# Transposing a token block with VectorE squares and 32 on-chip transfers instead of TensorE, from the fifth block on

## The chip, the core and the metric

The program runs on one core of a Trainium2 chip. The core has five engines that each work through their own queue in order and wait for each other through semaphores: PE (TensorE, matmuls), DVE (VectorE), ACT (ScalarE), POOL (GpSimd) and SP (SyncE, which here only issues DMAs). The metric is the device time of one execution in microseconds (us). Before the change the median of 3 runs is 1261.0 us (1260.62 to 1261.91).

## What is computed

Three layers over 8192 tokens of 192 channels (`D`), cut to what matters:

```
w   = softmax(weight_gen)            # per token: 8 heads x 7 taps
x1  = sum over k of w[..., k] * x[token - 6 + k]     # causal convolution, 24 channels a head
xn  = x1 / sqrt(mean(x1^2) + 1e-6) * rms_g
y   = (silu(xn @ w_gate) * (xn @ w_val)) @ w_out     # hidden size 1536
h   = y @ w_in                                       # hidden size 2048
out = (h * sigmoid(1.702 h)) @ w_out2
```

## The kernel before, in words

The 8192 tokens lie as 128 partitions of 64 consecutive tokens (a run of tokens per partition). A *block* is 4 tokens of every partition, 512 tokens in all; there are 16 blocks, 0 to 15. For a block the convolution works with tokens on the partitions (`conv_ops`, L215): 7 multiplications (L226) and 6 additions (L259) of 128x768 on DVE, then the sum of squares on ACT (L269, four instructions, called `sq` in the code), the reciprocal root on POOL (L274 and L276, `root`), and the scaling `xr = acc * ri` on DVE (L280) with a copy of the last 64 channels on ACT (L281).

The matmuls need channels on the partitions, so the block is transposed (`transpose_x`, L291). From block 3 on that is 16 PE transposes of 64x128 (L308) into two PSUM banks; `split` (L318) then reads PSUM and writes a high and a low part in float32r, on ACT (L324) and DVE (L325), for channels 0 to 127 (`xh`, `xl`) and for channels 128 to 191, which stand twice (`xsh`, `xsl`). All matmuls are made of high and low parts, and each takes 64 of the 128 partitions, upper and lower half in alternation, two at a time.

The work on PE is a list of *units*, written (layer, block, number). A unit (1, b, m) makes one 128-wide piece of gate and value of block b (12 a block); a unit (2, b, i) makes two pieces of the second hidden layer (8 a block). Each unit also holds "down" matmuls into the banks `a` and `b` with the hidden pieces of units before it. The hidden pieces come from PSUM over ACT (`silu`, and the high part `h`) and DVE (the product `p` in layer one, and the low part `l`, L435 and L455). From block 2 on the list reads, for each block b: (1, b, 4) to (1, b, 11), then (1, b+1, 0) to (1, b+1, 3), then (2, b, 0) to (2, b, 7). The low part of the even piece 2i of a layer-two unit i is used by the next unit, that of the odd piece by the one after (L698, L699).

When a PSUM bank passes from matmuls on one half of the partitions to matmuls on the other half, `handed` (L353) puts an empty instruction (a *word*) on POOL's queue that waits for the earlier matmul, and lets the later matmul wait for the word. A layer-two unit has six such words, the first before its fourth pair of matmuls.

The convolution of the coming block is handed out between the units. `some` (L579) records as much of a stream of DVE, ACT and POOL work as its cost, spread evenly until a due unit, asks for: half before the first low part of the unit (`second`), half before the second (`third`). The due unit hangs on `xt_at[b]`, the unit at which block b is transposed: L520 sets it to unit (1, b-1, 10). The convolution of block b starts at the transposition of block b-1 and is due two units before its own. The softmax weights are made for three blocks at once, so in front of blocks 4, 7, 10 and 13 stands a softmax: maximum and subtraction first, the exponential at unit (2, b-2, 2) (L668), and only then the rest of the softmax and the whole convolution (L678).

SP issues, per block, the load of the next x, and the two output DMAs of `Z` (L488), which scales the result of a block and adds its two halves (L495).

Of the kernel before, what the change touches and what calls it, by code (L numbers as in the profile page):

```python
# [18 lines left out]
P = 128  # L19
# [5 lines left out]
D = 192  # L25
DR = D - P
M1 = 12
# [3 lines left out]
BLOCKS = [4] * 16  # L31
# [6 lines left out]
SIG = 1.702  # L38
# [3 lines left out]
def gated_conv_mlp(ctx: ExitStack, tc: tile.TileContext, xp, wg, w1, wo1, w2, wo2, g, out):  # L42
    nc = tc.nc
    NB = len(BLOCKS)
    T0 = [sum(BLOCKS[:i]) for i in range(NB)]
    TM = max(BLOCKS)
    NM = TM * P
# [7 lines left out]
    xtp = ctx.enter_context(tc.tile_pool(name="xtp", bufs=2))  # L55
# [13 lines left out]
    gt = const.tile([P, 2], F32, name="gt")  # L69
# [81 lines left out]
    xrow = {}  # L151
    xT = {}
# [62 lines left out]
    def conv_ops(b):  # L215

        T = BLOCKS[b]
        Q = T * HEADS
        x = xch[b]
        wn = wn_of[b]  # L220
        xr = att.tile([P, T, 2 * P], F32, tag="xr", name=f"xr{b}")
        prod = xr.rearrange("p t c -> p (t c)")[:, 0:Q * GRP]
        ops = []

        def mul(eng, k, dst, j0=0, j1=T):
            eng.tensor_tensor(  # L226
                out=dst.rearrange("p (q g) -> p q g", g=GRP),
                in0=x[:, (k + j0) * D:(k + j1) * D].rearrange("p (q g) -> p q g", g=GRP),
                in1=wn[:, j0 * HEADS:j1 * HEADS, k:k + 1].to_broadcast([P, (j1 - j0) * HEADS, GRP]), op=ALU.mult)
        cost = 1.04 * Q * GRP + 70  # L230
        if b < 2:
            S = T // 2
            sums_of = [pacc.tile([P, NM], F32, tag=f"{n}{b}", name=f"{n}c_{b}") for n in "ab"]
            acc_of = [sums_of[j // S][:, (j % S) * D:(j % S + 1) * D] for j in range(T)]
        else:
            acc = att.tile([P, T, D], F32, tag="acc", name=f"acc{b}")
            acc_of = [acc[:, j] for j in range(T)]
        if b == 1:
            def tap(k):
                for i, ps in enumerate(sums_of):  # L240
                    tag = (("yh", "yl"), ("ysh", "ysl"), ("yh0", "yl0"))[k % 3][i]
                    pr = ytp.tile([P, NM], F32R, tag=tag, name=f"pr{k}_{i}").bitcast(F32)[:, :S * D]
                    mul(nc.gpsimd, k, pr, i * S, (i + 1) * S)
                    nc.tensor.matmul(ps[:, :S * D], ident, pr, start=k == 0, stop=k == TAPS - 1)
            ops += [(cost, lambda k=k: tap(k)) for k in range(TAPS)]
        elif b == 0:
            n = S * D

            def tap(k):
                for i, ps in enumerate(sums_of):  # L250
                    mul(nc.vector, k, prod[:, i * n:(i + 1) * n] if k else ps[:, :n], i * S, (i + 1) * S)
                for i, ps in enumerate(sums_of if k else ()):
                    nc.vector.tensor_tensor(out=ps[:, :n], in0=ps[:, :n], in1=prod[:, i * n:(i + 1) * n], op=ALU.add)
            ops += [(cost, lambda k=k: tap(k)) for k in range(TAPS)]
        else:
            total = acc.rearrange("p t d -> p (t d)")

            def add():
                nc.vector.tensor_tensor(out=total, in0=total, in1=prod, op=ALU.add)  # L259
            for k in range(TAPS):  # L260
                ops.append((cost, lambda k=k: mul(nc.vector, k, prod if k else total)))
                if k:
                    ops.append((cost, add))
        ss = sml.tile([P, T], F32, tag="ss", name=f"ss{b}")
        ri = sml.tile([P, T], F32, tag="ri", name=f"ri{b}")

        def sq():
            for j in range(T):
                nc.scalar.activation(out=xr[:, j, 0:D], in_=acc_of[j], func=AF.Square,  # L269
                                     accum_out=ss[:, j:j + 1])  # L270
        ops.append((1500, sq))

        def root():
            nc.gpsimd.tensor_scalar(out=ss, in0=ss, scalar1=1.0 / D, scalar2=1e-6,  # L274
                                    op0=ALU.mult, op1=ALU.add)
            nc.gpsimd.tensor_tensor(out=ri, in0=ss, in1=half[:, :T], op=ALU.pow)  # L276
        ops.append((500, root))

        def sc(j):
            nc.vector.tensor_scalar_mul(out=xr[:, j, 0:D], in0=acc_of[j], scalar1=ri[:, j:j + 1])  # L280
            nc.scalar.mul(out=xr[:, j, D:2 * P], in_=acc_of[j][:, P:D], mul=ri[:, j:j + 1])  # L281
        for j in range(T):
            ops.append((230, lambda j=j: sc(j)))
        xrow[b] = xr
        return ops

    def sums(b, nm):

        return [pacc.tile([P, NM], F32, tag=f"{n}{b % 2}", name=f"{n}{nm}{b}") for n in "ab"]

    def transpose_x(b, halves=False):  # L291

# [195 lines left out]
    def Z(b):  # L488
        N = BLOCKS[b] * P
        pa, pb = acc2.pop(b)  # L490
        za = zp.tile([P, NM], F32, tag="za", name=f"za{b}")
        zb = zp.tile([P, NM], F32, tag="zb", name=f"zb{b}")[0:DR]
        nc.scalar.mul(out=zb[:, :N], in_=pb[DR:P, :N], mul=1.0 / SIG)
        nc.scalar.mul(out=za[:, :N], in_=pa[:, :N], mul=1.0 / SIG)
        nc.vector.scalar_tensor_tensor(out=zb[:, :N], in0=pb[0:DR, :N], scalar=1.0 / SIG, in1=zb[:, :N],  # L495
                                       op0=ALU.mult, op1=ALU.add)
        c = T0[b] * P
        nc.sync.dma_start(out=out[0:P, c:c + N], in_=za[:, :N])
        nc.sync.dma_start(out=out[P:D, c:c + N], in_=zb[:, :N])
# [17 lines left out]

    xt_at = {0: -1, 1: pos[1, 1, 0], 2: pos[2, 1, PAIRS - 2]}
    for b in range(3, NB):
        xt_at[b] = pos[1, b - 1, M1 - 2]  # L520
    xt_by_pos = {v: k for k, v in xt_at.items()}
    group_of = {b0: gi for gi, (b0, b1) in enumerate(GROUPS)}


# [41 lines left out]
    def run_work(upto):  # L566
        for q in streams:
            while q and q[0][0] <= upto:
                q.popleft()[2]()
# [27 lines left out]
    with ExitStack() as order:  # L597
# [45 lines left out]
        for i, u in enumerate(units):  # L643
            kind, b, m = u
            if (kind, b, m) == (1, 2, 0):
                early.close()
                late = ctx.enter_context(tc.tile_pool(name="late", bufs=6))
                parts.append((late, late))
            run_work(i)
            late = []  # L650
            if i in xt_by_pos:
                split = transpose_x(nxt, nxt > 2)
                if nxt == 1:
                    split()
                else:
                    late.append(split)
                nxt += 1
                if nxt == 2:
                    start_at = pos[1, 1, 1]
                elif nxt < NB:  # L660
                    start_at = i
            if i == start_at:
                load_x(nxt)
                end = xt_at[nxt]
                gi = group_of.get(nxt)
                if gi is not None and gi >= 2:
                    pr, ex_hook, post_ops = softmax_ops(gi, sm[gi])
                    ex_at = i + 4 if gi == 2 else pos[2, nxt - 2, 2]  # L668
                    add_work(1, ex_at, pr)
                else:  # L670
                    add_work(1, end - 2, conv_ops(nxt))
                gi = group_of.get(nxt + 1)
                if gi is not None and gi >= 2:
                    sm[gi] = softmax_load(gi)
            if ex_hook and i == ex_at:
                ex_hook()
                ex_hook = None
                add_work(1, xt_at[nxt] - 2, post_ops + conv_ops(nxt))  # L678
            downs, after = [], []
            while pend and pend[0][0] <= i:  # L680
                _, D_, key = pend.popleft()
                d, f = D_(*key)
                downs.append(d)
                after += [f] if f else []
            second, third = (U1 if kind == 1 else U2)(b, m, lambda *ups: matmuls(ups, downs, kind == 2 and b < 2))
            todo = [share(k, i) / 2 for k in (0, 1)]
            some(todo)
# [67 lines left out]
```

## Time and profile before

| what | value |
|---|---|
| median of 3 runs | 1261.0 us |
| the profiled execution | 1261.79 us |
| its span, from the first to the last instruction | 1260.0 us |
| PE busy | 1225.8 us (97%) |
| DVE busy | 773.3 us (61%) |
| ACT busy | 662.7 us (53%) |
| POOL busy | 32.9 us (3%) |
| mean granted TensorE clock | 0.994 |
| chain that ended last | PE 89%, DVE 7%, ACT 2% |

The prediction works on the profiled execution, which is 0.8 us above the median. The busy time of PE counts an instruction to its end, and instructions overlap; PE's pace is read from the distance of starts. On DVE and ACT too, an instruction can start some 0.08 us before the end of the one ahead of it, so what one costs in a queue is the distance of starts.

### The profile page before, as it was taken

The numbers are of one execution on the slowest core, as the hardware profiler recorded it, in microseconds if no ns is written. First come the engines' busy times: TensorE is split into PE (matmuls) and PEld (weight loads), VectorE is DVE, ScalarE is ACT, GpSimd is POOL, SyncE is SP. The second block draws the span as 40 slices with busy tenths as digits, with TensorE's granted clock in tenths as the row PEclk, the third lists the DMA queues.
The fourth block names the chain that finished last, engine by engine and source line by source line (L and its number), as shares of the span: only waits on it lengthen the run. The fifth ranks groups of instructions, "written<-read, shape, count | busy, mean of one in ns | idle before, by whom it ended". The sixth has DMA issues, their size and how long they took to land.

```text
span 1260.0 us, 26630 instructions
## 1 busy us (share of the span) xinstructions
PE 1225.8 (97%) x10500; PEld 1073.5 (85%) x10500; DVE 773.3 (61%) x1270; ACT 662.7 (53%) x1345; POOL 32.9 (3%) x53
## 2 busy tenths in 40 slices
PE   5798999999999999999999999999999999999998
PEld 3676899988899998999998888888888898888886
DVE  8888957566746556674664667456466655645432
ACT  3565664564545456454545655445464554554553
POOL 4000000000000000000000000000000000000000
PEclk8899999999999999999999999999999999999999
DMA  5754502001000010100101010010100001000000
GB/s 196 228 180 151 164 27 67 33 1 45 2 26 32 1 45 1 45 1 2 56 2 45 1 45 2 1 56 1 45 2 17 29 1 46 1 14 2 1 14 13
DMA packets 16956, 51.70 MB, mean 41 GB/s; under 512 B 2112, under 2 KB 2496, under 8 KB 16832
## 3 DMA queue, kind: packets, MB, share of 16 engines
q1 hardware_dynamic: 16832, 50.01, 12.3%
q8 instruction: 82, 1.34, 0.4%
q14 instruction: 42, 0.34, 0.1%
HBM read 43.71 MB, written 6.29 MB: 40 GB/s over the span
## 4 chain that ended last, share of the span: by engine, by line
PE 89%; DVE 7%; ACT 2%; issue 1%; DMA 1%; SPq 0%; POOLq 0%; DVEq 0%
PE a L342 23%; PE ph L342 20%; PE pg L342 16%; PE b L342 16%; PE pv L342 13%; DVE l L435 1%; DVE p L431 1%; DVE dec_a L104 1%; DVE xr L226 1%; DVE dec_s L108 1%; DVE dec_s L98 1%; DMA x<-in_xp 1%; ACT h L432 0%; DVE zt L100 0%; DVE acc L259 0%
## 5 line engine op out<-in xcount | busy, mean ns | idle before, releaser
L342 PE MATMUL a<-h,o 64*128 64x512 f32 x1792 | 518.9, 392 | 0.4 <-POOLq L357 0.2
L342 PEld LDWEIGHTS a<-h,o 64*128 64x128 f32 x1792 | 329.3, 185 | 22.0 <-POOLq L357 1.1
L342 PE MATMUL a<-l,o 64*128 64x512 f32 x896 | 311.4, 393 | 2.2 <-DVE l L455 2.0
L342 PE MATMUL b<-l,o 64*128 64x512 f32 x896 | 311.0, 392 | 0.3 <-DVE l L435 0.3
L342 PE MATMUL b<-h,o 64*128 64x512 f32 x896 | 311.1, 393 | 0.0
L455 DVE TENSOR_TENSOR l<-p,h 128x512 fp32r<-128x512 f32 x256 | 176.0, 691 | 203.3 <-ACT p L449 202.3
L448 ACT ACTIVATE h<-ph 128x512 fp32r<-128x512 f32 x256 | 153.9, 601 | 227.0 <-PE ph L342 220.3
L342 PE MATMUL pv<-xh,w 64*128 64x512 f32 x768 | 242.8, 396 | 7.0 <-DVE p L431 6.6
L342 PE MATMUL pg<-xh,w 64*128 64x512 f32 x768 | 244.4, 396 | 1.3 <-ACT w L119 1.3
L342 PE MATMUL ph<-yh,w 64*128 64x512 f32 x1024 | 232.1, 391 | 0.0
L431 DVE TENSOR_TENSOR p<-p,pv 128x512 f32<-128x512 f32 x192 | 131.7, 686 | 144.7 <-PE a L342 100.4
L432 ACT CAST h<-p 128x512 fp32r<-128x512 f32 x192 | 119.1, 620 | 171.7 <-DVE p L431 171.7
L427 ACT ACTIVATE p<-pg 128x512 f32<-128x512 f32 x192 | 114.6, 597 | 161.2 <-PE pg L342 160.4
L435 DVE TENSOR_TENSOR l<-p,h 128x512 fp32r<-128x512 f32 x192 | 132.8, 692 | 98.5 <-ACT h L432 98.5
L342 PEld LDWEIGHTS a<-l,o 64*128 64x128 f32 x896 | 165.6, 185 | 18.3 <-DVE l L455 4.1
L342 PEld LDWEIGHTS b<-l,o 64*128 64x128 f32 x896 | 165.7, 185 | 13.5 <-DVE l L435 0.7
L342 PEld LDWEIGHTS b<-h,o 64*128 64x128 f32 x896 | 164.8, 185 | 9.8
L342 PEld LDWEIGHTS pv<-xh,w 64*128 64x128 f32 x768 | 140.4, 186 | 20.7 <-DVE p L431 9.7
L342 PEld LDWEIGHTS ph<-yh,w 64*128 64x128 f32 x1024 | 143.3, 185 | 15.1 <-POOLq L357 0.2
L449 ACT ACTIVATE p<-ph 128x512 f32<-128x512 f32 x256 | 154.0, 602 | 0.0
L342 PE MATMUL pv<-xl,w 64*128 64x512 f32 x384 | 150.9, 393 | 0.0
L342 PE MATMUL pg<-xl,w 64*128 64x512 f32 x384 | 150.5, 392 | 0.0
(101 smaller groups left out, 2134.9 us busy)
## 6 DMA issues: line engine op xcount, KB each, us to landing
x<-in_xp SPq DMA_DIRECT2D x15, 960.0 KB, 5.1
st<-in_w SPq DMA_DIRECT2D x20, 384.0 KB, 3.8
zt<-in_w SPq DMA_DIRECT2D x20, 384.0 KB, 3.4
st<-in_wo SPq DMA_DIRECT2D x14, 384.0 KB, 3.9
zt<-in_wo SPq DMA_DIRECT2D x14, 384.0 KB, 3.3
out_z<-za SPq DMA_DIRECT2D x16, 256.0 KB, 2.0
out_z<-zb SPq DMA_DIRECT2D x16, 128.0 KB, 2.3
wraw<-in_wg SPq DMA_DIRECT2D x4, 336.0 KB, 5.4
```

The lines of the kernel that those rows point to most:

```text
L98: nc.vector.tensor_scalar(out=t["s"], in0=hi, scalar1=-0x80000000, scalar2=4, op0=ALU.bitwise_and, op1=ALU.bitwise_or)
L104: nc.vector.scalar_tensor_tensor(out=ai, in0=ai, scalar=3, in1=t["s"], op0=ALU.logical_shift_left, op1=ALU.bitwise_or)
L108: nc.vector.tensor_single_scalar(t["s"], t["a"].bitcast(I32), -0x800000, op=ALU.bitwise_and)
L226: eng.tensor_tensor(out=dst.rearrange("p (q g) -> p q g", g=GRP), in0=x[:, (k + j0) * D:(k + j1) * D].rearrange("p (q g) -> p q g", g=GRP) ...
L342: ins = nc.tensor.matmul(ps[:, :N], w[rows], x[rows, :N], start=start, stop=stop)
L427: nc.scalar.activation(out=p[:, :N], in_=pg[:, :N], func=AF.Silu)
L431: nc.vector.tensor_tensor(out=p[:, :N], in0=p[:, :N], in1=pv[:, :N], op=ALU.mult)
L432: nc.scalar.copy(h[:, :N], p[:, :N])
L435: nc.vector.tensor_tensor(out=l[:, :N], in0=p[:, :N], in1=h[:, :N].bitcast(F32), op=ALU.subtract)
L448: nc.scalar.activation(out=h[:, :N], in_=ps[j][:, :N], func=AF.Silu, scale=SIG)
L449: nc.scalar.activation(out=p[:, :N], in_=ps[j][:, :N], func=AF.Silu, scale=SIG)
L455: nc.vector.tensor_tensor(out=l[:, :N], in0=p[:, :N], in1=h[:, :N].bitcast(F32), op=ALU.subtract)
```

## The change

From block 4 on the transposition leaves PE. `shuffle_x` lets DVE transpose the block in 32x32 squares with one instruction (128x768), from `xr` to a new tile `raw`, and then issues 32 DMAs on SP, each of 32 partitions by 128 elements (16 KB), that put the squares of `raw` in their places in `xl` and `xsl`. Tokens thereby stand in another order inside a block, by quarters of the 128 runs; `Z` puts them right when it writes, and its DVE addition becomes four of 64x128. `split` reads `xl` and `xsl` from SBUF and works in place, with two instructions of 128x512 on each engine in place of four of 128x256. The four ACT copies of the last 64 channels (L281) go.

The transposition is moved from unit (1, b-1, 10) to unit (1, b-1, 4), the first unit behind layer two of block b-2; `split` stays at (1, b-1, 10). With `xt_at` the due unit of the convolution moves: from (1, b-1, 8) to (2, b-2, 6). The load of the following x is issued ahead of the 32 transfers.

```
+    def shuffle_x(b):
+        T = BLOCKS[b]
...
+        raw = squares[0].tile([P, T * D], F32, tag="raw", name=f"raw{b}")
+        nc.vector.transpose(out=raw.rearrange("p (c j t) -> p j c t", j=T, t=Q),
+                            in_=xr[:, :, 0:D].rearrange("p j (c t) -> p j c t", t=Q))
+        raw = raw.rearrange("p (c n) -> p c n", n=T * Q)
+        full = P // Q
+        for q in range(full):
+            rows = slice(q * Q, (q + 1) * Q)
+            cols = slice(q * T * Q, (q + 1) * T * Q)
+            for c in range(D // Q):
+                dst = l if c < full else sl
+                for at in ((c,) if c < full else (c - full, c - full + 2)):
+                    nc.sync.dma_start(out=dst.bitcast(F32)[at * Q:(at + 1) * Q, cols], in_=raw[rows, c])
+        def split():
+            for c, (h_, l_) in enumerate(((h, l), (sh, sl))):
+                v = l_.bitcast(F32)[:, :N]
+                nc.scalar.activation(out=h_[:, :N], in_=v, func=AF.Identity, scale=gt[:, c:c + 1])
+                nc.vector.scalar_tensor_tensor(out=l_[:, :N], in0=v, scalar=gt[:, c:c + 1],
+                                               in1=h_[:, :N].bitcast(F32), op0=ALU.mult, op1=ALU.subtract)
+        return split
...
+        for k in range(BLOCKS[b] if b > 3 else 1):
+            z, v = (low[:, :, k], top[:, :, k]) if b > 3 else (zb[:, :N], pb[0:DR, :N])
+            nc.vector.scalar_tensor_tensor(out=z, in0=v, scalar=1.0 / SIG, in1=z, op0=ALU.mult, op1=ALU.add)
...
     for b in range(3, NB):
-        xt_at[b] = pos[1, b - 1, M1 - 2]
+        xt_at[b] = pos[1, b - 1, M1 - 2 if b < 4 else M1 - 8]
...
             if i in xt_by_pos:
-                split = transpose_x(nxt, nxt > 2)
+                if 2 < nxt < NB - 1:
+                    load_x(nxt + 1)
+                if nxt > 3:
+                    splits[pos[1, nxt - 1, M1 - 2]] = shuffle_x(nxt)
```

Three places show what this moves. In names, `l2_5_6` is the low part of piece 6 of layer two of block 5, `acc7` and `xr7` belong to the convolution of block 7.

On DVE, during layer two of block 5, the convolution of block 7 stands like this before:

```order
L455 TENSOR_TENSOR l2_5_5_6939<-p2_5_5_6937,h2_5_5_6938 128x512
L191 TENSOR_SCALAR mx4_6492<-mx4_6492 128x32
L192 RECIPROCAL mx4_6492<-mx4_6492 128x32
L195 TENSOR_TENSOR wraw4_5434<-wraw4_5434,mx4_6492 128x224
L226 TENSOR_TENSOR acc7_6873<-x7_6490,wraw4_5434 128x768
L455 TENSOR_TENSOR l2_5_6_6997<-p2_5_6_6995,h2_5_6_6996 128x512
L226 TENSOR_TENSOR xr7_6872<-x7_6490,wraw4_5434 128x768
L455 TENSOR_TENSOR l2_5_7_7002<-p2_5_7_7000,h2_5_7_7001 128x512
L259 TENSOR_TENSOR acc7_6873<-acc7_6873,xr7_6872 128x768
L455 TENSOR_TENSOR l2_5_8_7060<-p2_5_8_7058,h2_5_8_7059 128x512
```

and like this after the change:

```order
L488 TENSOR_TENSOR l2_5_5_6969<-p2_5_5_6967,h2_5_5_6968 128x512
L259 TENSOR_TENSOR acc7_6903<-acc7_6903,xr7_6902 128x768
L226 TENSOR_TENSOR xr7_6902<-x7_6210,wraw4_5184 128x768
L259 TENSOR_TENSOR acc7_6903<-acc7_6903,xr7_6902 128x768
L488 TENSOR_TENSOR l2_5_6_7032<-p2_5_6_7030,h2_5_6_7031 128x512
L226 TENSOR_TENSOR xr7_6902<-x7_6210,wraw4_5184 128x768
L259 TENSOR_TENSOR acc7_6903<-acc7_6903,xr7_6902 128x768
L488 TENSOR_TENSOR l2_5_7_7037<-p2_5_7_7035,h2_5_7_7036 128x512
L226 TENSOR_TENSOR xr7_6902<-x7_6210,wraw4_5184 128x768
L259 TENSOR_TENSOR acc7_6903<-acc7_6903,xr7_6902 128x768
L226 TENSOR_TENSOR xr7_6902<-x7_6210,wraw4_5184 128x768
L488 TENSOR_TENSOR l2_5_8_7095<-p2_5_8_7093,h2_5_8_7094 128x512
```

Between two low parts there stands one multiplication or addition before, and two or three after; the same rows stand in layer two of blocks 2, 8 and 11, for the convolutions of blocks 4, 10 and 13.

On ACT the sum of squares (L269) of block 7, which POOL's root waits for, stands before in the units of layer one of block 6:

```order
L427 ACTIVATE p1_6_6_7392<-pg6_6_7356 128x512
L269 ACTIVATE xr7_6872,ss7_6874<-acc7_6873 128x192 x4
L432 CAST h1_6_6_7393<-p1_6_6_7392 128x512
L427 ACTIVATE p1_6_7_7439<-pg6_7_7403 128x512
L432 CAST h1_6_7_7440<-p1_6_7_7439 128x512
```

and after the change in layer two of block 5, behind the last `silu` of unit (2, 5, 5):

```order
L481 ACTIVATE h2_5_11_7162<-ph5_11_7111 128x512
L482 ACTIVATE p2_5_11_7161<-ph5_11_7111 128x512
L269 ACTIVATE xr7_6902,ss7_6904<-acc7_6903 128x192 x4
L481 ACTIVATE h2_5_12_7226<-ph5_12_7179 128x512
L482 ACTIVATE p2_5_12_7225<-ph5_12_7179 128x512
```

The sum of squares is now part of a layer-two unit; the root on POOL is recorded in the same unit (2, 5, 5), behind that unit's words and ahead of those of unit (2, 5, 6). In the blocks without a softmax the sum of squares is recorded in unit (2, b-2, 3) and the root in (2, b-2, 5).

On SP there stand before, between two blocks:

```order
L498 DMA out_z<-za4_6279 128x512
L499 DMA out_z<-zb4_6280 64x512
L211 DMA x7_6490<-in_xp 128x1920
L498 DMA out_z<-za5_7349 128x512
L499 DMA out_z<-zb5_7350 64x512
L211 DMA x8_7564<-in_xp 128x1920
```

and after:

```order
L211 DMA x6_5140<-in_xp 128x1920
L314 DMA xl5_5143<-raw5_5146 32x128 x4
L314 DMA xsl5_5145<-raw5_5146 32x128 x4
L314 DMA xl5_5143<-raw5_5146 32x128 x4
L314 DMA xsl5_5145<-raw5_5146 32x128 x4
L314 DMA xl5_5143<-raw5_5146 32x128 x4
L314 DMA xsl5_5145<-raw5_5146 32x128 x4
L314 DMA xl5_5143<-raw5_5146 32x128 x4
L314 DMA xsl5_5145<-raw5_5146 32x128 x4
L158 DMA wraw4_5184<-in_wg 128x672
L537 DMA out_z<-za3_5282 128x512
L538 DMA out_z<-zb3_5283 64x512
```

The outputs of a block now stand behind 32 transfers, each of which needs `raw`, and the load of x ahead of them.

## Rows read from the trace of the kernel before

**Rows 1.** Windows of one block period: us, busy per engine, clock, DMA share, GB/s.
```profile
479.40:554.40 75.00, 75.00 (x660) 69.88 (x658) 49.62 (x79) 40.65 (x81) 1.34 (x2) 1.00 0.07 20
```

**Rows 2.** Timeline of PE around the transposes of one block: start us, us, instruction.
```profile
534.23 0.40 PE L342 MATMUL a<-l,o 64*128 64x512 f32 x1
534.42 0.21 PE L308 MATMUL ax<-ident,xr 64*128 64x64 f32 x1
...
535.20 0.39 PE L342 MATMUL pg<-xh,w 64*128 64x512 f32 x1
```

**Rows 3.** Timeline of DVE, softmax and convolution of block 7 during layer two.
```profile
489.77 0.62 DVE L188 TENSOR_REDUCE mx<-wraw 128x64 f32<-128x448 f32 x1 [1.39 <-ACT wraw L185]
...
490.65 0.56 DVE L192 RECIPROCAL mx<-mx 128x64 f32<-128x64 f32 x1
...
492.77 0.62 DVE L195 TENSOR_TENSOR wraw<-wraw,mx 128x448 f32<-128x448 f32 x1
493.31 0.38 DVE L188 TENSOR_REDUCE mx<-wraw 128x32 f32<-128x224 f32 x1
...
494.41 0.35 DVE L192 RECIPROCAL mx<-mx 128x32 f32<-128x32 f32 x1
494.80 0.39 DVE L195 TENSOR_TENSOR wraw<-wraw,mx 128x224 f32<-128x224 f32 x1
495.11 0.95 DVE L226 TENSOR_TENSOR acc<-x,wraw 128x768 f32<-128x768 f32 x1
495.98 0.68 DVE L455 TENSOR_TENSOR l<-p,h 128x512 fp32r<-128x512 f32 x1
496.58 0.95 DVE L226 TENSOR_TENSOR xr<-x,wraw 128x768 f32<-128x768 f32 x1
...
514.67 0.69 DVE L455 TENSOR_TENSOR l<-p,h 128x512 fp32r<-128x512 f32 x1
```

**Rows 4.** Timeline of PE in three units of that layer: first even low parts, first handover.
```profile
497.96 0.39 PE L342 MATMUL a<-l,o 64*128 64x512 f32 x1
...
502.38 0.39 PE L342 MATMUL a<-l,o 64*128 64x512 f32 x1
...
505.59 0.39 PE L342 MATMUL b<-h,o 64*128 64x512 f32 x1
```

**Rows 5.** Timeline of ACT, sum of squares of block 7, first and last.
```profile
524.75 0.36 ACT L269 ACTIVATE xr<-acc 128x192 f32<-128x192 f32 x1
...
526.04 0.19 ACT L269 ACTIVATION_READ_ACCUMULATOR xr<-acc 128x1 f32 x1
```

**Rows 6.** Timeline of POOL, root of block 7.
```profile
527.18 0.33 POOL L274 TENSOR_SCALAR ss<-ss 128x4 f32<-128x4 f32 x1 [77.02 <-PE a L342]
527.60 1.01 POOL L276 TENSOR_TENSOR ri<-ss,half 128x4 f32<-128x4 f32 x1
```

**Rows 7.** Timeline of SP: issues of two DMAs.
```profile
63.30 0.67 SPq L86 DMA_DIRECT2D st<-in_w  x1
...
524.25 0.34 SPq L498 DMA_DIRECT2D out_z<-za  x1
```

**Rows 8.** DMA issues of one kind: count, KB each, us to landing.
```profile
out_z<-za SPq DMA_DIRECT2D x16, 256.0 KB, 2.0
```

**Rows 9.** Timeline of ACT, the first instruction of `split`.
```profile
539.69 0.47 ACT L324 ACTIVATE xh<-ax,gt 128x256 fp32r<-128x256 f32 x1
```

**Rows 10.** Groups by line: the addition in `Z`.
```profile
L495 DVE SCALAR_TENSOR_TENSOR zb<-b,zb 64x512 f32<-64x512 f32 x16 | 10.9, 681 | 4.0 <-ACT zb L493 4.0
```

**Rows 11.** Timeline of PE, two of its waits; start, us, and idle time ahead.
```profile
34.64 0.49 PE L342 MATMUL pg<-xh,w 64*128 64x512 f32 x1 [1.34 <-ACT w L119]
...
43.15 1.31 PE L315 MATMUL ax<-ident,xr 128*128 128x128 f32 x4 [4.99 <-ACT xr L281]
```

**Rows 12.** Windows around those waits, columns as in rows 1, first of PE alone.
```profile
36.00:40.00 4.00, 2.16 (x20) 1.00 0.98 310
...
45.40:48.00 2.60, 2.60 (x13) 2.06 (x14) 2.29 (x5) 0.69 (x1) 0.00 (x0) 0.50 0.00 0
```

More of the change, by code (lines that the diff above doesn't have):

```diff
@@ L280, in sc @@
             nc.vector.tensor_scalar_mul(out=xr[:, j, 0:D], in0=acc_of[j], scalar1=ri[:, j:j + 1])
+            if b > 3:
+                return
             nc.scalar.mul(out=xr[:, j, D:2 * P], in_=acc_of[j][:, P:D], mul=ri[:, j:j + 1])
@@ L289, in sums @@
         return [pacc.tile([P, NM], F32, tag=f"{n}{b % 2}", name=f"{n}{nm}{b}") for n in "ab"]
+    Q = 32
+    squares = []
+    def shuffle_x(b):
+        T = BLOCKS[b]
+        N = T * P
+        xr = xrow.pop(b)
+        h, l, sh, sl = (xtp.tile([P, NM], F32R, tag=tag, name=f"{tag}{b}") for tag in ("xh", "xl", "xsh", "xsl"))
+        xT[b] = (h, l, sh, sl)
+        raw = squares[0].tile([P, T * D], F32, tag="raw", name=f"raw{b}")
[17 more added lines that the diff above has]
+        return split
     def transpose_x(b, halves=False):
@@ L492, in Z, with of @@
         zb = zp.tile([P, NM], F32, tag="zb", name=f"zb{b}")[0:DR]
[L493 to L496, printed above, removed]
+        order, like = ("p (q j t) -> p q j t", "p (j q t) -> p q j t") if b > 3 else ("p (j q t) -> p j q t",) * 2
+        def of(v, how):
+            return v[:, :N].rearrange(how, j=BLOCKS[b], t=Q)
+        nc.scalar.mul(out=of(zb, like), in_=of(pb[DR:P], order), mul=1.0 / SIG)
+        nc.scalar.mul(out=of(za, like), in_=of(pa, order), mul=1.0 / SIG)
+        top, low = of(pb[0:DR], order), of(zb, like)
+        for k in range(BLOCKS[b] if b > 3 else 1):
+            z, v = (low[:, :, k], top[:, :, k]) if b > 3 else (zb[:, :N], pb[0:DR, :N])
+            nc.vector.scalar_tensor_tensor(out=z, in0=v, scalar=1.0 / SIG, in1=z, op0=ALU.mult, op1=ALU.add)
         c = T0[b] * P
@@ L519, in gated_conv_mlp @@
     for b in range(3, NB):
-        xt_at[b] = pos[1, b - 1, M1 - 2]
+        xt_at[b] = pos[1, b - 1, M1 - 2 if b < 4 else M1 - 8]
     xt_by_pos = {v: k for k, v in xt_at.items()}
+    splits = {}
     group_of = {b0: gi for gi, (b0, b1) in enumerate(GROUPS)}
@@ L648, in gated_conv_mlp @@
                 parts.append((late, late))
+                squares.append(ctx.enter_context(tc.tile_pool(name="squares", bufs=1)))
             run_work(i)
-            late = []
+            late = [splits.pop(i)] if i in splits else []
             if i in xt_by_pos:
-                split = transpose_x(nxt, nxt > 2)
-                if nxt == 1:
-                    split()
-                else:
-                    late.append(split)
+                if 2 < nxt < NB - 1:
+                    load_x(nxt + 1)
+                if nxt > 3:
+                    splits[pos[1, nxt - 1, M1 - 2]] = shuffle_x(nxt)
+                else:
+                    split = transpose_x(nxt, nxt > 2)
+                    late += [split] if nxt > 1 else []
+                    if nxt == 1:
+                        split()
                 nxt += 1
@@ L662, in gated_conv_mlp @@
             if i == start_at:
-                load_x(nxt)
+                if nxt < 4:
+                    load_x(nxt)
                 end = xt_at[nxt]
```

## The prediction

> **What bounds the kernel now.** I read the windows first, one block period at a time. In the period from 479.40 to 554.40 PE is busy for 75.00 of 75.00 us, at full clock, DVE for 49.6 and ACT for 40.7 [rows 1]. The periods around it are alike, so PE's own instructions are the time there. A change can gain only what it takes out of PE's queue, and loses whatever makes PE wait; DVE or ACT work alone changes nothing until a matmul waits for it. So I then read the timeline of PE where the transposes stand, and the timeline of DVE, ACT and POOL in the stretch where the new order of work differs.
>
> **What goes from PE.** A pair of matmuls starts every 0.23 us. Around the transposes the last matmul of the unit before starts at 534.23, the first transpose at 534.42, and the second pair of the next unit at 535.20 [rows 2]. Without them that second pair would stand two steps behind 534.23, at 534.69. The 16 transposes cost 0.51 us, not their summed durations, since they overlap. Twelve blocks (4 to 15) make 12 x 0.51 = 6.1 us. Nothing else leaves PE. The ACT copies (L281) and the smaller `split` leave ACT, which is not late anywhere in the period: gain 0.
>
> **What the earlier due unit costs.** The due unit of the convolution moves from (1, b-1, 8) to (2, b-2, 6). For blocks without a softmax the start moves as well, and 18 units stay 18. For blocks 4, 7, 10 and 13 the convolution can't start before the exponential at unit (2, b-2, 2), so ten units shrink to four of layer two, and the DVE rows after the change show two or three convolution instructions between two low parts. I add up DVE's queue for block 7 from 489.77, where the exponential releases it, with slots (distance of starts) from [rows 3].
>
> First the softmax: reduction and scaling 0.88 (489.77 to 490.65); reciprocal 0.60 (0.56 and 0.04 until the dependent one, as 494.41 to 494.80 for 0.35); the 448-wide multiplication 0.54; the smaller reduction and scaling 0.62 (493.31 to 494.41 less a low part of 0.60 is 0.50, and 0.12 for the dependence); reciprocal 0.30; low part 4, 0.60; the 224-wide multiplication 0.31. Then two multiplications of 0.87 (495.11 to 495.98) and low part 5, 0.60. That is 6.19, so 495.96.
>
> Then addition, multiplication, addition. A multiplication behind an addition overwrites what that one reads, and the next addition needs it, so I take the whole 0.95 and 0.03 for such a neighbour, 0.98, and 0.87 in front of a low part. The trace has no such neighbours; 0.87 throughout is the lower bound. 0.98 + 0.98 + 0.87: low part 6 starts at 498.79 and ends at 499.48. The matmul that uses it started at 497.96 [rows 4]. PE waits 1.5 us.
>
> Low part 6 (0.60), multiplication 0.98, addition 0.87, low part 7 (0.60), then 0.98 + 0.98 + 0.87: low part 8 starts at 504.67, ends at 505.36. Its matmul was due at 502.38 [rows 4], now 1.5 later at 503.9. PE waits another 1.5 us; it is 3.0 late.
>
> Low part 8 (0.60), addition 0.98, multiplication 0.87, low part 9 (0.60), and the last addition ends at 508.67. Now the sum of squares follows on ACT at once: 524.75 to 526.23, 1.48 us [rows 5], so 510.15. Then the root on POOL: 527.18 to 528.61, 1.43 us [rows 6], so 511.58, and 0.15 for three hand-overs between engines, an estimate from the 0.09 between the two rows on POOL: 511.73. Behind the root on POOL's queue stand the words of unit (2, 5, 6). Its first matmul that needs one stood at 505.59 [rows 4]. A root that waits holds every word behind it, and so PE: what ran at 505.59 runs at 511.73. The block loses 6.1 us in all, the two waits for low parts included, and the third wait is 3.1 us. Behind it DVE has caught up: its next scalings need 0.5 us, and unit (2, 5, 6) brings its low parts 6 us later than before. Before the change the root stood in layer one and found the sum of squares long done (POOL waited 77 us for PE, not for ACT [rows 6]).
>
> Four such blocks with the same rows: 4 x 6.1 = 24.4 us. With 0.87 throughout, six neighbours by 0.11 less, it is 5.5 a block and 21.8; with 0.3 more of waits in ACT 25.6.
>
> **The other blocks.** There the sum of squares is recorded two units ahead of the root, and is done when POOL gets there. The root then runs behind the last word of unit (2, b-2, 5), which waits for the 13th of 19 pairs: 12.5 x 0.23 and 0.39 for the matmul, 3.3 us into a unit of 4.4 (497.96 to 502.38). With 1.43 for the root it ends 0.3 into the next unit, whose first word is wanted behind three pairs, at 0.7. I take 0; the bound is 0.4 us in eight blocks, 3 us.
>
> **The transfers.** The low part of the last layer-two piece starts at 514.67 [rows 3], and DVE is free 0.60 later, at 515.27. The transpose has no row; between 0.3 and 1.9 (a third and twice the 0.95 of a 128x768 multiplication) I take 0.95, the row that moves as many elements: 516.2. SP issues in 0.34 to 0.67 us [rows 7]. 32 x 0.34 = 10.9, and the last lands 2.0 later [rows 8]: 529.1. `split` starts at 539.69 [rows 9] and shifts with PE like everything here, so 10.6 us are to spare, and it costs 0; with 0.67 an issue the spare is 0. The output DMAs behind them come some 5 us later, and their tiles are next written when layer one of the following block has ended. The load of x goes out ahead and earlier than before: 0.
>
> **`Z`.** One addition of 0.68 [rows 10] becomes four of a quarter of the width, between 0.7 and 2.7 in all. DVE has room for it, except behind the last matmul of the program: 0.2, at most 2.0.
>
> **The sum.** 1261.79 - 6.1 + 24.4 + 0.2 = 1280.3 for the profiled execution; the median stands 0.8 lower, so 1279.5 us. With the bounds of these terms 1276 to 1284.
>
> **Rivals.**
>
> *DVE takes it in.* No matmul waits, and only the transposes go: 1261.0 - 6.1 + 0.2 = 1255.1, faster. For it: DVE is idle for a third of the period [rows 1], and 1.39 us ahead of the softmax [rows 3]. Against it: that idle time lies in all units, the added work in four, where a unit of 4.4 us gets five convolution slots and two low parts, 5.8 us. It decides if the slots were some 0.3 us shorter than the trace has them.
>
> *Only the low parts are late.* If the words of the next unit don't stand behind the root, or the root comes in time, a block loses 3.0, not 6.1: 1261.0 - 6.1 + 0.2 + 12.0 = 1267.1. For it: in no row of before does a word wait for a root. Against it: POOL's queue is in order, and so is the recording.
>
> *The clock falls in the third wait.* After 1.34 us without a matmul the clock stayed at 1.00 (2.4 GHz), after 4.99 us it stood at 0.50 (1.2 GHz) from 43.15 to 48.0 at least [rows 11, 12]. The wait of 3.1 us lies between them. A fall costs half of 4.85 us, 2.4 a block: 1279.5 + 4 x 2.4 = 1289. The Trainium skill (TensorE: Matmul & The Clock Gate, Part 1: The HAM clock gate) says that the clock goes down when TensorE has been idle long enough and comes back only under work; the two rows agree, and none has a wait of this length.
>
> *The transfers are late.* If an issue of 32 partitions costs more than 0.67 us, `split` waits in all twelve blocks, with ACT and DVE behind it: at 0.8 an issue 25.6 + 2.0 from 516.2 is 543.8, 4.1 late, 12 x 4.1 = 49 us and a time of 1329. For it: these are 16 KB each, where [rows 8] moves 256 KB. Against it: the trace issues in 0.34, and transfers overlap. The Trainium skill (DMA: Bandwidth & Descriptors, Rules for kernel authors) advises against many small transfers, which under 64 KB are mostly overhead, and for one large one; no row here shows 32 in a series.
>
> **How the numbers follow.** Forecast 0.60; only the low parts 0.13; the clock falls 0.12; DVE takes it in 0.08; transfers late 0.05; the last 0.02 lies near no change. The range holds the forecast and the second and third case, 0.85: 1264 to 1292; the forecast's own is 1276 to 1284. 0.2% is 2.5 us, about what a measurement tells from no change. Faster 0.09 (DVE takes it in, and a little), same 0.03, slower 0.88.
>
> **What the profile after would show.** Right: PE waits for DVE's low parts twice and for a word on POOL once, in layer two of blocks 2, 5, 8 and 11, about 1.5, 1.5 and 3 us, nowhere else; periods of 74.5 us in the other blocks and of 80.6 in these; POOL's L274 waits for ACT there; `split` follows the last `h` without waiting for a DMA. Wrong: no wait of PE in these units; a wait of the same size in all blocks, which would be the transfers or the root of the blocks without a softmax; `split` waiting for a DMA; or a clock under 1.00 after the third wait.

## The result, and the profile after

The changed kernel takes 1277.2 us (median of 4 runs, 1276.2 to 1278.1) beside 1261.0 us for the kernel before, a ratio of 1.0127 (95% interval 1.0110 to 1.0145). It is slower, by 16.2 us; 18.5 were forecast (1279.5). The profiled execution took 1278.1 us, its span is 1276.3, so that it compares with 1260.0 in the table above.

First the waits of PE, the five largest sums in the whole changed kernel (line of kernel.py, releaser, us in total, times, longest):

```profile
PE a L375 <- DVE l L488: 9.9, 10, 1.2
PE ax L348 <- ACT xr L283: 8.9, 2, 4.5
PE ac L244 <- POOL pr L226: 8.0, 1, 8.0
PE b L375 <- POOLq L390: 8.0, 4, 2.7
PE pv L375 <- DVE p L464: 6.6, 7, 2.0
```

The kernel before has this row for the low parts:

```profile
PE a L342 <- DVE l L455: 2.0, 3, 1.0
```

So seven of the ten waits for low parts of layer two (L455 before, L488 now) are new, and all four waits of `b` for a word on POOL. The other rows stand in the first blocks, as before.

The windows of two block periods (from one scaling in `Z` to the next; PE busy, clock, DMA share, GB/s) answer to [rows 1]. The first holds the convolution of block 7, the second one of a block without a softmax:

```profile
453.43:533.05 79.62, 75.65 (x644) 1.00 0.08 25
607.47:682.02 74.55, 74.55 (x644) 1.00 0.11 32
```

The same periods took 74.98 on average before (74.94 to 75.07). Periods without a softmax now take 74.48 on average (74.4 to 74.6), 0.50 less; the three of blocks 7, 10 and 13 take 79.62, 79.85 and 79.59.

DVE during the squeezed convolution of block 7 (start us, us, instruction, and in brackets idle time and who ended it), to be held against [rows 3]:

```profile
494.63 0.62 DVE L188 TENSOR_REDUCE mx<-wraw 128x64 f32<-128x448 f32 x1 [1.39 <-ACT wraw L185]
...
500.73 0.95 DVE L259 TENSOR_TENSOR acc<-acc,xr 128x768 f32<-128x768 f32 x1
501.71 0.96 DVE L226 TENSOR_TENSOR xr<-x,wraw 128x768 f32<-128x768 f32 x1
502.71 0.96 DVE L259 TENSOR_TENSOR acc<-acc,xr 128x768 f32<-128x768 f32 x1
503.58 0.69 DVE L488 TENSOR_TENSOR l<-p,h 128x512 fp32r<-128x512 f32 x1
...
509.50 0.69 DVE L488 TENSOR_TENSOR l<-p,h 128x512 fp32r<-128x512 f32 x1
...
512.57 0.95 DVE L259 TENSOR_TENSOR acc<-acc,xr 128x768 f32<-128x768 f32 x1
```

DVE does not idle from 494.63 to 513.52. Neighbours of the convolution start 0.98 and 1.00 apart, and 0.87 ahead of a low part, as taken. PE in the same stretch, three matmuls that waited, to be held against [rows 4]:

```profile
504.32 0.50 PE L375 MATMUL a<-l,o 64*128 64x512 f32 x1 [1.13 <-DVE l L488]
510.24 0.49 PE L375 MATMUL a<-l,o 64*128 64x512 f32 x1 [1.10 <-DVE l L488]
515.49 0.49 PE L375 MATMUL b<-h,o 64*128 64x512 f32 x1 [1.74 <-POOLq L390]
```

Take the reduction as the common zero (489.77 before, 494.63 now, 4.86 apart). The three matmuls then stand 1.50, 3.00 and 5.04 us later than before; 1.5, 3.0 and 6.1 were forecast. What the third waits for is seen on ACT and POOL (to [rows 5] and [rows 6]):

```profile
513.61 0.36 ACT L269 ACTIVATE xr<-acc 128x192 f32<-128x192 f32 x1 [0.33 <-DVE acc L259]
...
514.92 0.19 ACT L269 ACTIVATION_READ_ACCUMULATOR xr<-acc 128x1 f32 x1
```

```profile
515.19 0.19 POOL L274 TENSOR_SCALAR ss<-ss 128x4 f32<-128x4 f32 x1 [79.60 <-ACT xr L269]
515.47 1.01 POOL L276 TENSOR_TENSOR ri<-ss,half 128x4 f32<-128x4 f32 x1
```

The matmul starts at 515.49, when the power (L276) has just begun, not when it has ended at 516.48. So the word did not wait for the running power.

Ahead of the prediction it was said that the same DVE rows stand in layer two of block 2, for the convolution of block 4. They do not: low part 8 has two convolution instructions ahead of it there, and low part 9 three, where block 7 has three and two. PE waits for only one low part, and longer for the word:

```profile
273.05 0.50 PE L375 MATMUL a<-l,o 64*128 64x512 f32 x1 [1.10 <-DVE l L488]
...
284.17 0.79 PE L375 MATMUL b<-h,o 64*128 64x512 f32 x1 [2.66 <-POOLq L390]
```

The matmul behind the root is as late all the same: it starts 20.81 us behind the reduction that opens the rest of the softmax, beside 20.86, 20.97 and 20.86 for blocks 7, 10 and 13. The third wait takes up what the waits for low parts have left.

The clock after the third wait: first the window behind the first such wait (block 4), then behind the one of block 7:

```profile
284.00:290.00 6.00, 5.83 (x28) 0.50 0.13 52
515.50:521.50 6.00, 6.00 (x51) 1.00 0.09 36
```

In the first of the four events (an event is the squeezed convolution of block 4, 7, 10 or 13) PE sat idle for 2.66 us in the third wait, against 1.74, 1.83 and 1.74 in the other three, and the granted clock fell to 1.2 GHz (0.50) until about 290. Behind the other three it stayed at 1.00 (2.4 GHz).

Last the transfers, on SP, the last 32 ahead of a `split` (4 in a row of the trace), and that `split` on ACT:

```profile
525.86 3.17 SPq L314 DMA_DIRECT2D xl<-raw  x4
529.07 2.49 SPq L314 DMA_DIRECT2D xsl<-raw  x4
...
545.12 2.49 SPq L314 DMA_DIRECT2D xsl<-raw  x4
```

```profile
549.20 0.72 ACT L319 ACTIVATE xh<-xl,gt 128x512 fp32r<-128x512 f32 x1
549.83 0.71 ACT L319 ACTIVATE xsh<-xsl,gt 128x512 fp32r<-128x512 f32 x1
```

Neither waits for a DMA. But four issues take 2.53 us from row to row, 0.63 each. The last one starts at 547.02, and a landing takes 1.8 us from the start of the issue (median on the page), so the last square is there at 548.8. ACT starts on `xsl` at 549.83. Spare is 1.0 us here, not the 10.6 of the prediction; by the landings in the trace it is 0.2 to 2.4 us over the twelve blocks.

### The profile page after: what moved, and what is told of

Read it like the earlier page. It is cut to its first block, busy times and chain, and to the rows that moved or that the text cites. A ratio compares the mean times of both kernels' runs of the same rounds, so it can differ in the third digit from the quotient of the medians.

```text
span 1276.3 us, 26762 instructions
## 1 busy us (share of the span) xinstructions
PE 1227.6 (96%) x10308; PEld 1149.5 (90%) x10308; DVE 782.8 (61%) x1294; ACT 652.7 (51%) x1273; POOL 32.4 (3%) x53
## 4 chain that ended last, share of the span: by engine, by line
PE 83%; DVE 10%; ACT 4%; issue 3%; DMA 0%; POOL 0%; POOLq 0%; DVEq 0%
PE a L375 22%; PE ph L375 18%; PE pg L375 15%; PE b L375 14%; PE pv L375 14%; DVE xr L226 2%; DVE l L488 1%; DVE l L468 1%; DVE p L464 1%; DVE dec_a L104 1%; DVE acc L259 1%; ACT h L481 1%; DVE dec_s L108 1%; DVE dec_s L98 1%; ACT p L482 1%
## 5 line engine op out<-in xcount | busy, mean ns | idle before, releaser
L488 DVE TENSOR_TENSOR l<-p,h 128x512 fp32r<-128x512 f32 x256 | 175.8, 689 | 197.8 <-ACT p L482 196.6
L375 PE MATMUL ph<-yh,w 64*128 64x512 f32 x1024 | 240.8, 393 | 0.0
L375 PEld LDWEIGHTS ph<-yh,w 64*128 64x128 f32 x1024 | 149.6, 185 | 9.8 <-POOLq L390 0.2
L375 PE MATMUL ph<-yl,w 64*128 64x512 f32 x512 | 156.7, 392 | 0.0
```

Of the source, the lines that this page charges most:

```text
L375: ins = nc.tensor.matmul(ps[:, :N], w[rows], x[rows, :N], start=start, stop=stop)
L488: nc.vector.tensor_tensor(out=l[:, :N], in0=p[:, :N], in1=h[:, :N].bitcast(F32), op=ALU.subtract)
```

## The experiments

Times are medians; "before" is the kernel before on the same chip, 1261.2 to 1261.6 us in these sets. Each expectation was written before its run.

**Only the due unit is moved, in the kernel before (before_due).**

```
-                end = xt_at[nxt]
+                end = pos[1, nxt - 1, 4] if nxt in (4, 7, 10, 13) else xt_at[nxt]
...
-                add_work(1, xt_at[nxt] - 2, post_ops + conv_ops(nxt))
+                add_work(1, end - 2, post_ops + conv_ops(nxt))
```

> The kernel before, transposes on PE and everything else as it is, but for blocks 4, 7, 10 and 13 the due unit of the convolution is (2, b-2, 6), as in the changed kernel. Theory (the early due unit alone makes the loss): 5.04 a block as in the changed kernel's block 7, 1261.0 + 4 x 5.04 = 1281.2, and 2.6 for each of the four waits in which the clock falls (one in the changed kernel): 1281 to 1286. Rival (the loss needs the transposition on DVE or the transfers): under 1266.

Measured 1286.7 us, ratio 1.0206 (1.0189 to 1.0223). PE's waits, and the clock in the 8 us behind each of the four third waits:

```profile
PE b L342 <- POOLq L357: 10.8, 4, 2.8
```

```profile
284.00:292.00 8.00, 8.00 (x70) 1.00 0.00 0
514.00:522.00 8.00, 8.00 (x56) 0.79 0.01 2
746.00:754.00 8.00, 8.00 (x59) 0.79 0.00 1
977.00:985.00 8.00, 7.77 (x66) 1.00 0.01 2
```

With neither the DVE transposition nor a transfer in the kernel the waits appear in the same units, as for block 4 in the changed kernel: one for a low part (1.1 us) and a longer one for a word (2.65 to 2.78). The stretches with an event and a full clock are 5.1 and 5.2 us longer than before (80.12 against 74.98 for block 13), the two with a fall 6.7 and 6.8. That is 23.8 for the four, beside 23.5 in the changed kernel: the due unit alone makes the loss. The median lies 0.7 above the expected range; the profiled execution, with two falls of the clock, is the fastest of the four.

**The root one unit later (root_later).**

```
-                add_work(1, xt_at[nxt] - 2, post_ops + conv_ops(nxt))
+                *conv, root, s0, s1, s2, s3 = conv_ops(nxt)
+                add_work(1, xt_at[nxt] - 2, post_ops + conv)
+                add_work(1, xt_at[nxt] - 1, [root, s0, s1, s2, s3])
```

> The changed kernel, but in blocks 4, 7, 10 and 13 the root and the scalings behind it are due one unit later, (2, b-2, 7), so that the root stands behind the words of unit (2, b-2, 6). Theory (the third wait is the root that waits for the sum of squares ahead of those words): waits of b for POOL words in layer two gone, the two waits for low parts stay; 1277.2 - 4 x 2.04 - 2.6 (no fall of the clock) = 1266.4, 1265.5 to 1269. Rival (PE would be late there anyway, since the low parts are): within 2 us of 1277. Rival (the transposition comes later, and with it the transfers and the split): 1270 to 1278, with new waits for xl or xh at (1, b, 0).

Measured 1264.9 us, ratio 1.0029 (1.0018 to 1.0040). No wait of `b` for POOL is left in layer two; in each event one wait of 1.1 us for a low part stays, beside shorter ones:

```profile
PE a L375 <- DVE l L488: 6.4, 9, 1.1
```

Periods with an event are 77.0, 2.6 over the others. The third wait is the root that waits for the sum of squares ahead of the words. The time came out 1.5 below the expectation and 0.6 below its range: the stream due at (2, b-2, 6) is shorter by the root and the scalings, so that its instructions are spread more thinly. In the event of block 7, for example, two instructions of the convolution stand ahead of low part 6 where three stood. So 2.6 are lost where 3.0 were.

**The power twice (double_pow).**

```
             nc.gpsimd.tensor_scalar(out=ss, in0=ss, scalar1=1.0 / D, scalar2=1e-6,
                                     op0=ALU.mult, op1=ALU.add)
+            if b in (4, 7, 10, 13):
+                nc.gpsimd.tensor_tensor(out=ri, in0=ss, in1=half[:, :T], op=ALU.pow)
             nc.gpsimd.tensor_tensor(out=ri, in0=ss, in1=half[:, :T], op=ALU.pow)
```

> The changed kernel with the power of the root (1.01 us on POOL) issued twice, with the same result, in blocks 4, 7, 10 and 13. Asks what of the root holds the words behind it. Theory (a word passes one power that is running, as at 515.49, but the second power does not start until the first has ended, so the words stand behind the start of the second): third wait 1.0 longer, 1277.2 + 4 x 1.0 = 1281.2, and up to 2.6 more for each further fall of the clock: 1280 to 1289. Rival (a word passes whatever computes and stands only behind the wait of the first root instruction for ACT): 1277 again. Rival (the prediction's: a word stands behind the end of the whole root, and the profile only shows POOL late): 1281 as well, but then the matmul starts behind the end of the second power, not beside it.

Measured 1284.9 us, 7.8 over the changed kernel. POOL and PE at block 7's root:

```profile
516.93 0.19 POOL L274 TENSOR_SCALAR ss<-ss 128x4 f32<-128x4 f32 x1 [79.60 <-ACT xr L269]
517.21 1.01 POOL L277 TENSOR_TENSOR ri<-ss,half 128x4 f32<-128x4 f32 x1
518.29 1.01 POOL L278 TENSOR_TENSOR ri<-ss,half 128x4 f32<-128x4 f32 x1
```

```profile
518.33 0.79 PE L377 MATMUL b<-h,o 64*128 64x512 f32 x1 [2.82 <-POOLq L392]
```

The matmul starts 0.04 behind the start of the second power: the word waits for all POOL instructions ahead of it but the last to end, and does not wait for that one. In the other three events it is 0.03. A wait 1.1 longer four times is 4.4; the clock, which falls in three of the four events where it fell in one, adds 2.6 and 1.7 in the profiled execution.

**The exponential in layer one (early_exp).**

```
-                    ex_at = i + 4 if gi == 2 else pos[2, nxt - 2, 2]
+                    ex_at = i + 4
```

> The changed kernel, but for blocks 4, 7, 10 and 13 the exponential is recorded four units behind the transposition of the block before, in layer one, as it already is for block 2, so that the convolution is spread over ten or more units again, not four. Theory (the whole loss is the squeezed convolution, and the transposes had cost PE about 0.48 us a block): no wait for low parts or words in layer two; 1261.0 - 12 x 0.48 + 0.2 = 1255.4 us, 1254 to 1257. Rival (the DVE transposition and the 32 transfers cost PE time of their own): 1261 or more. Rival (an exponential in layer one makes PE wait for ACT, which then lacks 3 to 4 us in a unit of 3.3): 1 to 3 us in four blocks, 1259 to 1267.

Measured 1260.5 us, ratio 0.9994 (0.9985 to 1.0004): the loss is gone, but 5 us of the expected gain are missing; the second rival was right. Where block 4's exponential stands next to the end of layer one of block 2, PE waits for ACT:

```profile
255.69 0.49 PE L375 MATMUL ph<-yh,w 64*128 64x512 f32 x1 [1.49 <-ACT p L460]
```

That stretch is 3.3 us longer than before, and the periods of blocks 7, 10 and 13 are 75.2 and 75.3, 0.8 over the others: 3.3 + 3 x 0.8 = 5.7. An exponential with its two table loads (1.28 us each) and 0.77 of its own holds ACT for 3.4 us (456.06 to 459.44 for block 7), which the place at (2, b-2, 2) hid. The 0.8 arise at the `split` of the block before, which now stands behind that exponential on ACT (467.03): the first matmul that needs it starts 0.51 behind the matmul ahead of it, where a pair otherwise starts every 0.23, and those with `xl` and `xsh` lose the rest.

```profile
467.29 0.39 PE L375 MATMUL a<-l,o 64*128 64x512 f32 x1
467.80 0.49 PE L375 MATMUL pg<-xh,w 64*128 64x512 f32 x1
```

**The exponential at the start of layer two, and the root later (exp0_root).** Beside the edit of root_later:

```
-                    ex_at = i + 4 if gi == 2 else pos[2, nxt - 2, 2]
+                    ex_at = i + 4 if gi == 2 else pos[2, nxt - 2, 0]
```

> The changed kernel with two edits for blocks 4, 7, 10 and 13: the exponential at unit (2, b-2, 0), two units earlier, and the root due one unit later. DVE then has six units of 4.4 = 26.4 us for 15.3 us of softmax and convolution and twelve low parts of 0.60, 22.5 in all. Theory (only the squeeze lost time; the transposes cost PE 0.48 a block): no waits in layer two, 1261.4 - 12 x 0.48 = 1255.6, 1254.5 to 1258. Rival (the exponential with its table loads, 3.3 us of ACT, makes PE wait wherever two layers meet, as for block 4 with the early exponential): 0.8 to 3.5 in each of four blocks, 1259 to 1270.

Measured 1263.0 us, ratio 1.0011 (1.0001 to 1.0020). The rival again: ACT is held for 3.4 us where the hidden pieces of the first units are due, the pieces and DVE's low parts come late, and PE waits for one:

```profile
489.57 0.50 PE L375 MATMUL a<-l,o 64*128 64x512 f32 x1 [1.19 <-DVE l L488]
```

Each such period is 76.5 to 76.7, 2.1 over the others. Adding up DVE's queue (22.5 of 26.4 us) was not enough: its input was late.

**The softmax a block ahead (ahead).** For block 4 the edit does what exp0_root does; for the later softmaxes its core is:

```
+                elif ahead is not None and ahead >= 4:
+                    pr, ex_hook, post_ops = softmax_ops(ahead, sm[ahead])
+                    ex_at = pos[2, nxt - 2, 2]
+                    c = conv_ops(nxt)
+                    add_work(1, ex_at, c[:2] + pr + c[2:9])
```

> The changed kernel, but the softmax for blocks 7 to 9, 10 to 12 and 13 to 15 is made one block earlier, during the convolution of blocks 6, 9 and 12, with the exponential at unit (2, b-3, 2), in layer two; blocks 7, 10 and 13 then have 18 units for the convolution, as the others. Block 4 has the exponential at (2, 2, 0) and the root a unit later. Theory (squeeze alone): no waits behind unit (1, 2, 4), 1255.6 us, 1254.5 to 1258. Rival (the convolutions of blocks 6, 9 and 12 now carry the softmax and are late themselves, or the exponential holds ACT): 1 to 3 us in each of three blocks, 1258 to 1265.

Measured 1299.0 us, ratio 1.0301 (1.0285 to 1.0316): neither of the two came true. The waits of PE and DVE name the cause:

```profile
DVE mx L175 <- DMA wraw<-in_wg: 47.1, 4, 14.9
...
PE b L375 <- DVE l L468: 35.7, 5, 11.9
```

The load of the softmax weights stood behind the 32 transfers on SP's queue, 20 us of issuing. The maximum that needs it stood at the head of DVE's queue, and PE waited up to 11.9 us for a low part behind it. In the changed kernel that load stands in the same place, but is needed a block later.

**The transposition one unit later (shuffle_plus1)**, on top of the early exponential:

```
-        xt_at[b] = pos[1, b - 1, M1 - 2 if b < 4 else M1 - 8]
+        xt_at[b] = pos[1, b - 1, M1 - 2 if b < 4 else M1 - 7]
...
-                end = xt_at[nxt]
+                end = xt_at[nxt] - (1 if nxt > 3 else 0)
...
-                add_work(1, xt_at[nxt] - 2, post_ops + conv_ops(nxt))
+                add_work(1, end - 2, post_ops + conv_ops(nxt))
```

> The kernel with the early exponential, but the transposition and the 32 transfers start one unit later, at (1, b-1, 5); the convolution's due unit and the split stay. Theory (32 issues of 0.62 us leave 0.4 to 1.3 us to spare, and the split feeds PE 0.5 us ahead of need): the last transfer is 1.9 to 2.9 us late, PE waits 1.4 to 2.4 in twelve blocks: 17 to 29 us over the early exponential's time, about 1276. Rival (10.6 us to spare, as in the prediction): no difference. Rival (issues of SP overlap more when nothing else is on the queue, so some us to spare): 0 to 5 us.

Measured 1301.6 us, 41 over the early exponential. `split` now waits for the transfers, in all twelve blocks:

```profile
632.29 0.72 ACT L319 ACTIVATE xh<-xl,gt 128x512 fp32r<-128x512 f32 x1 [1.09 <-DMA xl<-raw]
634.77 0.72 ACT L319 ACTIVATE xsh<-xsl,gt 128x512 fp32r<-128x512 f32 x1 [1.75 <-DMA xsl<-raw]
```

and behind it the clock is at half (windows of PE, columns as above):

```profile
634.00:636.00 2.00, 0.89 (x6) 1.00 0.59 97
637.00:640.00 3.00, 3.00 (x17) 0.50 0.16 61
641.00:642.00 1.00, 1.00 (x12) 1.00 0.08 16
```

A period is 78.4, 3.9 over the 74.5 without a wait, in the profiled execution, which is the slowest of the four. Some 3.4 us at half clock are 1.7 of it; the other 2.2 lie in the expected 1.4 to 2.4, but the clock was not in the expectation, and so the time lies above its range. The transfers were hidden by less than one unit.

**25 transfers in place of 32, one unit later (fewer_plus1).** Those of the first half of `xsl` go first, then `xl`, and one copy makes the second half:

```
+        for q, c in [(q, c) for cs in ((4, 5), (0, 1, 2, 3)) for q in range(full) for c in cs]:
...
+        nc.sync.dma_start(out=sl.bitcast(F32)[DR:P, :N], in_=sl.bitcast(F32)[0:DR, :N])
```

> The early exponential with the transposition at (1, b-1, 5), as before, but 25 transfers in place of 32: 8 that fill the first half of xsl go first, then the 16 of xl, then one of 64 partitions by 512 elements that copies the first half of xsl to the second. Theory (SP's 0.62 us an issue sets when the last transfer lands): the last lands 7 x 0.62 = 4.3 us earlier, the split doesn't wait for a DMA, PE waits under 0.5 us and the clock stays: 1260 to 1264, some 40 us under the kernel with 32. Rival (the landing of what was transferred, not the issue, is the limit, or the last copy has to wait for the eight before it): 1275 to 1302.

Measured 1261.5 us, ratio 1.0001 (0.9991 to 1.0010): 40 us come back. SP's rows (this view begins behind the first of the eight for `xsl`):

```profile
597.46 4.38 SPq L312 DMA_DIRECT2D xsl<-raw  x7
601.94 11.09 SPq L312 DMA_DIRECT2D xl<-raw  x16
613.07 0.60 SPq L313 DMA_DIRECT2D xsl<-xsl  x1
```

The same bytes land in time with seven issues fewer: the number of issues on SP, 0.6 to 0.7 us each, sets the pace.

**The softmax a block ahead, mended (softmax_ahead).** It has the lines shown for `ahead`, for blocks from 5 on; block 4 keeps its transposes on PE and its late due unit, so that eleven blocks change, and `sc` and `Z` test for `b > 4`. What differs:

```
+                gi = group_of.get(nxt + 2, 0)
+                if gi > 3:
+                    sm[gi] = softmax_load(gi)
                 if 2 < nxt < NB - 1:
                     load_x(nxt + 1)
-                if nxt > 3:
+                if nxt > 4:
                     splits[pos[1, nxt - 1, M1 - 2]] = shuffle_x(nxt)
...
+                rest = post_ops + conv_ops(nxt) if nxt < 5 else c[9:14] + post_ops + c[14:]
+                add_work(1, xt_at[nxt] - 2, rest)
```

> As the run with the softmax one block ahead, mended in three places. The softmax weights are loaded ahead of the 32 transfers and not behind them (there DVE's maximum waited for them at the head of its queue, and PE up to 11.9 us). Block 4 keeps PE's transposes and its late due unit, so that eleven blocks, 5 to 15, change. The rest of the softmax is recorded between the sum of squares and the root. Theory (the squeeze was the whole loss, the transposes cost PE 0.48 us a block): no wait of PE from layer two of block 2 on, all periods from block 5 on 74.4 to 74.6, and 1261.5 - 11 x 0.48 = 1256.2 us, 1255.3 to 1257.5, faster than before by 0.4%. Rival (DVE's work cannot be placed without making some low part late, wherever it goes): 1 to 2 us in each of three blocks, 1259 to 1262.

Measured 1254.9 us (1254.4 to 1255.4), ratio 0.9949 (0.9937 to 0.9962): faster than the kernel before, by 6.3 us, and 0.4 below the expected range. Windows of two periods, the second with the convolution of block 13:

```profile
445.58:520.16 74.58, 74.58 (x644) 1.00 0.09 27
892.52:967.14 74.62, 74.62 (x644) 1.00 0.09 27
```

From layer two of block 2 on no wait for a low part is left, and for a word only one of 0.2 us at the end, as before. With the squeeze out of the way the transposes' gain stands alone: behind the first 205 us the profiled execution is 5.5 us shorter than that of before, 0.50 for each of the eleven blocks. The other 1.9 between the two spans lie in the first 205 us, which the edit does not touch.

**The same with 25 transfers (softmax_ahead_25).** The edit is that of fewer_plus1.

> The same kernel with 25 transfers in place of 32 (those of xsl first, its second half filled by one copy). Theory (32 transfers just land in time for the split, 0.4 to 1.3 us ahead): the same time, within 0.2%. Rival (in some blocks the split does wait a little for the last transfer, unseen between two of ACT's instructions): 1 to 4 us less.

Measured 1255.1 us, ratio 0.9947 (0.9933 to 0.9961): no difference. 32 transfers land in time for `split`, by 0.6 us at the least in the run above.

## Why the prediction was right, and which terms were not

*What goes from PE: 12 x 0.51 = 6.1.* Measured 0.50 in each of eleven periods, and 0.24 for block 15 in the longer stretch behind them: 5.7. softmax_ahead gives it by itself.

*The queue of DVE.* Right to 0.1 us in every step for block 7. Counted from the reduction, low part 6 starts at 9.02 by the sum and at 8.95 in the trace, low part 8 at 14.90 and 14.87, and the last addition ends at 18.90 and 18.89. The 0.98 for dependent neighbours, which no row of before had, is what they take (0.98 to 1.00).

*The two low parts: 1.5 and 3.0.* Measured 1.50 and 3.00 for block 7. That all four blocks have the same rows was wrong: for block 4 one of the two waits is missing. It changes nothing in the loss, since the third wait makes up for it.

*The root ahead of the words: 3.1.* The mechanism was right (root_later takes it away), its size was not: 2.04 for block 7. The step "a root that waits holds every word behind it" took the word to stand behind the end of both POOL instructions. The root itself ended where the sum has it, 21.85 behind the reduction (21.96 by the sum). But the word stands behind the start of its last instruction (515.47 and 515.49; with a second power 518.29 and 518.33), which makes the wait 1.0 less. The Trainium skill (GPSIMD Engine Reference, 2.1 Instruction dispatch) says that an instruction's completion holds back what waits on its semaphore, but not the next Pool instruction. These rows agree for an empty instruction behind a power. The second power did start only behind the end of the first (1.08 behind its start, and it took 1.01).

*The clock.* A rival by itself (2.4 a fall, four falls), it came in one event of four: the stretch with block 4's event is 7.9 us longer than before, against 5.1 to 5.4 of the other three over the periods beside them, 2.6 for the fall. That this makes up for much of what the root cost less is chance: before_due had two falls, double_pow three.

*The transfers.* Hidden, as forecast, but for a wrong reason. The row of 0.34 an issue was the wrong one of [rows 7]; 0.63 is next to the upper bound of 0.67, at which the prediction itself had no time to spare, and the least that was spare is 0.2. The rival of late transfers stood closer than its 0.05 said: one unit later it cost 3.9 a block. The Trainium skill (DMA: Bandwidth & Descriptors, Issuing engines are not separate DMA queues) calls the time in which a sequencer initiates a DMA usually small beside the DMA itself. Here 32 issues are 20 us beside landings of 1.8, and the measurement decides.

*The other blocks, and `Z`.* Taken at 0 and 0.2. The periods of the other blocks lost nothing: they are shorter by the 0.50 above. From the last scaling in `Z` to the end it takes 5.0 us in both profiles. The transposition on DVE takes 0.97 (0.95 taken).

The sum on the profiled executions: -5.7 for the transposes; 5.1 + 5.4 + 5.1 for blocks 7, 10 and 13 and 7.9 for block 4, 23.5 in all (24.4 forecast); and -1.4 in the first 205 us. That is 16.4, beside 16.3 of the spans. The -1.4 is no gain of the change: that stretch took 207.2 us in the profiled execution of before and 205.5 in before_due, which has the same instructions there. So the forecast was right by its mechanism, and the number is closer (16.2 for 18.5) than its terms: the root was put about 1.0 too high in each of four blocks, 4 us in all, and one fall of the clock, not in the forecast, gave 2.6 of them back.

## What to carry to other kernels

A transposition that leaves the busy engine is a gain only if what it needs stays as early as it has to be: add up the queue between the release of its input and the new due time before moving it, and move the release (here the softmax) with it. Before a wait goes into an in-order queue, list what stands behind it: the words behind a root, and one load behind 32 small transfers, each held PE for microseconds. For many small transfers count the issues, not the bytes.

## What the runs showed of the hardware

- An issue of a transfer of 32 partitions by 512 bytes took SP 0.63 us in a series; 1.8 us to land.
- A transposition of 128x768 in 32x32 squares on DVE took 0.97 us, about as long as a multiplication of that size (0.95).
- An empty instruction on POOL, behind a power of 1.01 us, let its matmul go 0.02 to 0.05 us behind the start of that power, in all twelve events of the changed kernel, before_due and double_pow.
- The clock does not follow from the length of one idle time of PE alone. Of eight waits with 2.65 to 2.83 us idle (one in the changed kernel, four in before_due, three in double_pow) five came with a fall to 1.2 GHz, and three kept the full 2.4 GHz. None of three with 1.74 to 1.83 idle had a fall. But all twelve blocks of shuffle_plus1 had one, where the longest idle time was 0.7 to 1.75, and PE was busy for 0.89 of 2.00 us ahead of the one shown. What decides it stays open. A fall cost 1.5 to 2.6 us.
